# Filter by FFT and gated feed-forward on one core: the taps of the convolution converted earlier from a buffer of their own, batch 0's last transform stage three iterations sooner

## The chip, the cores and the metric

The kernel runs on one core of a Trainium2 chip. The core has TensorE (PE in the profile, its weight loads PEld), VectorE (DVE), ScalarE (ACT), GpSimd (POOL) and SyncE (SP, which here only issues DMAs); ACT issues some DMAs as well. The metric is the device time of one execution in microseconds (us), lower is better. Before the change it was 1565.62 us, the median of three runs (1565.36 to 1567.5).

## The reference

All data are float32. A batch of 8 sequences of 3136 positions with 256 channels is filtered in the frequency domain, and the result goes through a feed-forward layer whose hidden values are gated by a sigmoid of their own convolution over three positions.

```python
batch, seq, dim, d_ff, kernel = 8, 3136, 256, 1024, 3
X = np.fft.rfft(x, axis=1)
y = np.fft.irfft(X * (filt_r + 1j * filt_i)[None], n=seq, axis=1)

h = np.maximum(y @ w_in, 0.0)
hp = zero-padded h, one position on each side
conv_out = sum(conv_w[k][None, None, :] * hp[:, k:k + seq, :] for k in range(3))
gate = 1.0 / (1.0 + np.exp(-conv_out))
out = (h * gate) @ w_out
```

`w_in`, `conv_w` and `w_out` arrive as float64 and are turned into float32 on the core; `w_in` and `w_out` are then split in a high and a low part.

## The kernel before

The transform of length 3136 = 112 x 28 is done as matrix products. There are two stretches of work.

**The forward stretch** is one loop over `i` (`for i in range(NI)`) with a software pipeline. A batch is cut into 14 pieces p, so there are 112 pieces; call the piece number k (0 to 111). In iteration `i` each engine gets, in this order of the code:

- `filt` of k = i - 17: three products on DVE (L354, L355, L356) and a sum on POOL (L358) that makes the tile z;
- `third` of k = i - 19: PE, z times the table `i1_sb` (L365);
- `first` of k = i - 1: PE, the input piece x times `s1_sb` (L319), for i up to 112;
- `second` of k = i - 16: PE (L342; for the last piece of a batch L345);
- `turn` of k = i - 15: four transposes on PE (L330);
- ACT then copies the PSUM results out: `store` of the third stage (L309, followed by the DMA L311 that ACT issues, which writes it to DRAM), `keep` of the first (L323), `turned_rows` (L335);
- one step of the conversion of the convolution's taps (`csteps`, i = 26 to 33) or of the weights (`wsteps`, from i = 35 on, eight blocks of ten steps). A step is one DVE operation of `to_f32` (L160 to L172), the POOL sum at its end (L174), or the split (ACT L146, POOL L152).

From iteration `done` = 116 on, batch 0's **last stage** runs in the same loop: a load of two rows from DRAM (L198), the product with `m2_sb` on PE (L215) one iteration later, and one more iteration later `last_out`: the high part on ACT (L146) and the low part on DVE (L149), written to the tiles y. There are 14 such pieces, so the loop has 133 iterations. `done` also is the iteration where the pools of the input and of the conversion are closed, so the weights have to be finished by then.

**The gated stretch** follows (iteration m). `inner` (six matmuls, L177 to L179) needs all of batch 0's y. Then come `relu` (ACT L458, L460), `conv` (DVE L465, L466), `gate` (ACT L470, DVE L471), `split_g` (ACT L146, POOL L152), and six iterations later `project` (L491 to L493). The last stage of the other seven batches is spread over this stretch. `inner` writes one of four PSUM buffers `ps_h`, which is free again when L471 of its iteration has read it.

The order on PE, ACT, DVE and POOL is the order of the code (`manual_schedule`). SP's queue is in the order that the scheduler gives it. The DMAs of SP and ACT share eight completion semaphores, and an issue waits for the DMA that used its semaphore before.

Input pieces are loaded seven ahead (`XBUFS`). The filter tables and `i1_sb` are loaded piece by piece in iterations 10 to 23 of SP's order (L252 to L256), the taps (L274) in iteration 26, the first two blocks of weights (L269) in iteration 30. The taps' buffer is one of the two `raw` buffers that the blocks of weights use. The loop gives `csteps` eight turns, of which the first three pass without an operation; so five of the eight operations of `to_f32` run on the taps.

## Time and profile before

| | |
|---|---|
| median of three runs | 1565.62 us |
| the profiled execution's own time | 1568.01 us |
| its span, first to last instruction | 1566.2 us |
| PE busy | 1541.9 us (98%) |
| DVE busy | 1288.1 us (82%) |
| ACT busy | 1246.0 us (80%) |
| POOL busy | 704.9 us (45%) |
| mean granted TensorE clock | 0.997 |
| first `inner` of the gated stretch | 377.9 us after the span's start |

A row of a timeline has the start, the duration, engine, line, operation, the tiles (out<-in) and shapes, the count, and in brackets the idle time of the engine just before, with what ended it. A row by windows has for each engine the busy time in that window, then the granted clock (PEclk), the busy share of the DMA engines and what they moved. L12 is line 12 of the kernel.

### The profile page before, as it was taken

Reading aid. Unit: us, or ns where it says so; the run is one execution under the profiler, and the core shown is the slowest. Engines: PE = TensorE matmul, PEld = TensorE weight load, DVE = VectorE, ACT = ScalarE, POOL = GpSimd, SP = SyncE. Lnnn points to the kernel's source line nnn. Section 1 sums busy time; section 2 is a strip of 40 time slices with the busy share of each in tenths; the row PEclk is TensorE's granted clock in tenths of the full one; section 3 lists DMA queues with packets and bytes.
Section 4 is the critical chain, followed back from the end, with each engine's and each line's share of the span. In section 5 each row is a group of like instructions: output and inputs, shape, how many; then the busy total and the mean of one; then the engine's idle time right before and its main releaser. Section 6 shows DMA issues by size and latency. Waiting matters only on the chain.

```text
span 1566.2 us, 27791 instructions
## 1 busy us (share of the span) xinstructions
PE 1541.9 (98%) x10320; PEld 1419.9 (91%) x10320; DVE 1288.1 (82%) x1976; ACT 1246.0 (80%) x2274; POOL 704.9 (45%) x624
## 2 busy tenths in 40 slices
PE   8899999998999999999999999999999999999998
PEld 7677777776999999999999999999999999999998
DVE  3778877888888888888888888888888888888887
ACT  5655555556888888888888888888888888888887
POOL 3345555553444444444444444444444444444444
PEclk9999999999999999999999999999999999999999
DMA  9855555443111011111110111111011110100001
GB/s 233 247 168 167 167 173 168 139 134 106 30 54 48 29 49 48 48 48 45 46 39 22 48 54 48 48 48 48 31 42 48 48 51 28 48 24 24 24 24 48
DMA packets 89062, 115.24 MB, mean 74 GB/s; under 512 B 7400, under 2 KB 60168, under 8 KB 88928
## 3 DMA queue, kind: packets, MB, share of 16 engines
q1 hardware_dynamic: 74592, 87.77, 18.3%
q10 hardware_dynamic: 14336, 25.70, 5.8%
q8 instruction: 82, 1.34, 0.4%
q14 instruction: 52, 0.43, 0.1%
HBM read 62.06 MB, written 51.38 MB: 72 GB/s over the span
## 4 chain that ended last, share of the span: by engine, by line
PE 95%; DMA 2%; DVE 2%; ACT 1%; POOL 0%; issue 0%; SPq 0%; ACTq 0%; POOLq 0%; DVEq 0%
PE ps_h L178 12%; PE ps_h L179 12%; PE ps_h L177 11%; PE po L491 11%; PE po L493 11%; PE po L492 11%; PE ps L365 6%; PE pp L342 6%; PE ps_h L215 6%; PE ps L319 5%; PE ps L330 3%; DMA x<-in_x 1%; DVE y L149 1%; PE ps L215 1%; ACT y L146 1%; PE pp L345 0%
## 5 line engine op out<-in xcount | busy, mean ns | idle before, releaser
L152 POOL TENSOR_TENSOR g<-t,g 128x448 fp32r<-128x448 f32 x448 | 517.8, 1156 | 667.6 <-ACT g L146 264.3
L491 PE MATMUL po<-wo,g 128*128 128x256 f32 x1568 | 441.5, 282 | 0.0
L493 PE MATMUL po<-wo,g 128*128 128x256 f32 x1568 | 433.8, 277 | 0.0
L492 PE MATMUL po<-wo,g 128*128 128x256 f32 x1568 | 433.4, 276 | 0.0
L465 DVE SCALAR_TENSOR_TENSOR t<-ps_h,cw,t 128x448 f32<-128x448 f32 x448 | 305.6, 682 | 83.9 <-ACT t L460 73.2
L178 PE MATMUL ps_h<-y,wi 128*128 128x450 f32 x896 | 330.4, 369 | 4.5 <-DVE y L149 4.5
L177 PE MATMUL ps_h<-y,wi 128*128 128x450 f32 x896 | 328.6, 367 | 3.7 <-ACT y L146 2.0
L179 PE MATMUL ps_h<-y,wi 128*128 128x450 f32 x896 | 328.8, 367 | 0.0
L466 DVE SCALAR_TENSOR_TENSOR t<-ps_h,cw,t 128x448 f32<-128x448 f32 x448 | 306.5, 684 | 16.0
L460 ACT ACTIVATE t<-ps_h,cw 128x448 f32<-128x448 f32 x448 | 285.2, 637 | 43.2 <-ACT ps_h L458 2.6
L491 PEld LDWEIGHTS po<-wo,g 128*128 128x128 f32 x1568 | 294.8, 188 | 7.0
L492 PEld LDWEIGHTS po<-wo,g 128*128 128x128 f32 x1568 | 294.3, 188 | 5.7
L493 PEld LDWEIGHTS po<-wo,g 128*128 128x128 f32 x1568 | 294.5, 188 | 0.0
L458 ACT ACTIVATE ps_h<-ps_h 128x450 f32<-128x450 f32 x448 | 251.8, 562 | 31.5 <-PE ps_h L179 26.7
L471 DVE TENSOR_TENSOR t<-ps_h,t 128x448 f32<-128x448 f32 x448 | 275.3, 615 | 0.1
L470 ACT ACTIVATE t<-t 128x448 f32<-128x448 f32 x448 | 255.0, 569 | 12.1 <-DVE t L466 10.9
L146 ACT ACTIVATE g<-t 128x448 fp32r<-128x448 f32 x448 | 254.5, 568 | 0.2 <-DVE t L471 0.2
L358 POOL TENSOR_TENSOR z<-u,v 120x512 f32<-120x512 f32 x112 | 157.8, 1409 | 187.2 <-DVE v L356 165.0
L179 PEld LDWEIGHTS ps_h<-y,wi 128*128 128x128 f32 x896 | 168.3, 188 | 13.9
L177 PEld LDWEIGHTS ps_h<-y,wi 128*128 128x128 f32 x896 | 170.1, 190 | 12.0 <-ACT y L146 3.0
L178 PEld LDWEIGHTS ps_h<-y,wi 128*128 128x128 f32 x896 | 168.3, 188 | 13.6 <-DVE y L149 6.8
L149 DVE TENSOR_TENSOR y<-ps_h,y 128x448 fp32r<-128x448 f32 x98 | 103.2, 1053 | 75.8 <-ACT y L146 75.8
(53 smaller groups left out, 1658.1 us busy)
## 6 DMA issues: line engine op xcount, KB each, us to landing
x<-in_x SPq DMA_DIRECT2D x112, 224.0 KB, 4.9
b_dram<-sb ACTq DMA_DIRECT2D x112, 224.0 KB, 2.5
br<-b_dram SPq DMA_DIRECT2D x112, 224.0 KB, 2.6
out<-ot SPq DMA_DIRECT2D x27, 896.0 KB, 4.1
raw<-in_w_in SPq DMA_DIRECT2D x8, 256.0 KB, 4.0
raw<-in_w_out SPq DMA_DIRECT2D x8, 256.0 KB
t_sb<-in_fr SPq DMA_DIRECT2D x15, 112.0 KB
t_sb<-in_fi SPq DMA_DIRECT2D x14, 112.0 KB
```

Source lines behind the costliest of these rows:

```text
L146: nc.scalar.activation(dst, src, AF.Copy)
L152: nc.gpsimd.tensor_tensor(out=dst, in0=src, in1=hi.bitcast(F32), op=ALU.subtract)
L177: nc.tensor.matmul(ps, lhsT=wh, rhs=rh, start=start, stop=False, **kw)
L178: nc.tensor.matmul(ps, lhsT=wh, rhs=rl, start=False, stop=False, **kw)
L179: nc.tensor.matmul(ps, lhsT=wl, rhs=rh, start=False, stop=stop, **kw)
L460: nc.scalar.activation(t, h[:, 1:SUB + 1], AF.Copy, scale=cw[:, 1, f:f + 1])
L465: nc.vector.scalar_tensor_tensor(out=t, in0=h[:, 0:SUB], scalar=cw[:, 0, f:f + 1], in1=t, op0=ALU.mult, op1=ALU.add)
L466: nc.vector.scalar_tensor_tensor(out=t, in0=h[:, 2:SUB + 2], scalar=cw[:, 2, f:f + 1], in1=t, op0=ALU.mult, op1=ALU.add)
L471: nc.vector.tensor_mul(t, h[:, 1:SUB + 1], t)
L491: nc.tensor.matmul(o, lhsT=gh[:, sl], rhs=wo[0][:, f], start=first, stop=False, skip_group_check=True)
L492: nc.tensor.matmul(o, lhsT=gh[:, sl], rhs=wo[1][:, f], start=False, stop=False, skip_group_check=True)
L493: nc.tensor.matmul(o, lhsT=gl[:, sl], rhs=wo[0][:, f], start=False, stop=last, skip_group_check=True)
```

## The change

- The taps get a buffer of their own (`rawc`); their load moves from iteration 26 to iteration 8 of SP's order, and their conversion from iterations 26 to 33 to 14 to 21. All eight operations of `to_f32` now run on them.
- The blocks of weights 0 and 1 are loaded in iterations 25 and 27 instead of 30, and their conversion starts at i = 30 instead of 35.
- `done` goes from 116 to 113: batch 0's last stage starts three iterations sooner, and the loop has 130 iterations. The third stage of the last piece (k = 111) no longer fits in it. It is put into the gated stretch behind `inner` of m = 1, with PSUM from `ps_h`; its z, its two table slices (`i1_end`, one more DMA) and its output buffer are kept in a small pool `rest`.
- The tiles `a` go from three buffers to two and `sb` from four to three.

```diff
+    END = NP * B - 1
+    rest = ctx.enter_context(tc.tile_pool(name="rest", bufs=1))
+    i1_end = rest.tile([120, 2, 112], F32, name="i1_end")
+    z_end = rest.tile([120, 2, D], F32, name="z_end")
+    sb_end = rest.tile([112, 2, D], F32, name="sb_end")
+
+    def store(b, p, ps, st):
+        nc.scalar.activation(st, ps, AF.Copy)
+        v = b_dram[b].rearrange("n (r g) d -> (n r) g d", g=G)
+        nc.scalar.dma_start(out=v[:, 2 * p:2 * p + 2], in_=st)
+
+    def third(ps, tables, z):
+        for j in range(2):
+            nc.tensor.matmul(ps[:, j], lhsT=tables[:, j], rhs=z[:, j], start=True, stop=True)
...
         def convert_conv():
             n = 3 * NF
-            raw = cv.tile([128, 2, 512], I32, name="raw")
-            nc.sync.dma_start(out=raw[:, 0, 0:2 * n], in_=conv_w)
-            for _ in range(3):
-                yield
             em = cv.tile([128, 2, 512], I32, name="em", bufs=1)
-            yield from to_f32(cw.rearrange("p k f -> p (k f)"), raw[:, 0, 0:2 * n], em[:, 0, 0:n], em[:, 1, 0:n])
+            yield from to_f32(cw.rearrange("p k f -> p (k f)"), raws.pop("cw"), em[:, 0, 0:n], em[:, 1, 0:n])
...
-            r = fp.tile([112, 2, D], F32, name="a", bufs=3)
+            r = fp.tile([112, 2, D], F32, name="a", bufs=2)
...
-            z = fp.tile([120, 2, D], F32, name="z", bufs=3)
+            z = z_end if (b, p) == at(END) else fp.tile([120, 2, D], F32, name="z", bufs=3)
...
-        done = NP * B + 4
+        done = NP * B + 1
...
                 if i == 8:
                     nc.sync.dma_start(out=eye_sb, in_=eye)
                     nc.sync.dma_start(out=s2_sb, in_=s2[:, 0:120])
+                    raws["cw"] = cv.tile([128, 6 * NF], I32, name="rawc", bufs=1)
+                    nc.sync.dma_start(out=raws["cw"], in_=conv_w)
...
+                if i == 24:
+                    nc.sync.dma_start(out=i1_end, in_=i1[:, G - 2:G])
...
-                    store(*at(m - 4), pt)
+                    store(*at(m - 4), pt, fp.tile([112, 2, D], F32, name="sb", bufs=3))
...
-                if 26 <= i < 34:
+                if 14 <= i < 22:
                     next(csteps, None)
-                if i == 30:
-                    load_weights(0)
-                    load_weights(1)
-                if i >= 35:
+                if i in (25, 27):
+                    load_weights((i - 25) // 2)
+                if i >= 30:
                     next(wsteps, None)
...
+            if m == 1:
+                pt = ps_h.tile([128, 512], F32, name="ps_h")[0:112].rearrange("p (n d) -> p n d", n=2)
+                third(pt, i1_end, z_end)
             if a := at(m - PLAG):
                 project(*a)
...
+            if m == 1:
+                store(B - 1, NP - 1, pt, sb_end)
```

What the change does to the order on three queues is shown below; the line numbers of the changed kernel differ (L160 to L174 are the same in both; L354 to L356 became L359 to L361, L304 became L315, L269 became L285, L365 became L238).

DVE at iterations 29 to 31, before. The three rows of a `filt` are followed by one row of a conversion; `em<-raw 128x24` is the taps.

```order
L354 TENSOR_TENSOR u<-pp,t_sb 120x512
L355 TENSOR_TENSOR v_98<-pp,t_sb 56x512
L356 TENSOR_TENSOR v_98<-pp,t_sb 56x512
L160 TENSOR_SCALAR em<-raw 128x24
L354 TENSOR_TENSOR u<-pp,t_sb 120x512
L355 TENSOR_TENSOR v_99<-pp,t_sb 56x512
L356 TENSOR_TENSOR v_99<-pp,t_sb 56x512
L162 TENSOR_SCALAR em<-raw 128x24
```

And now; `em<-raw 128x512` is block 0 of the weights.

```order
L359 TENSOR_TENSOR u<-pp,t_sb 120x512
L360 TENSOR_TENSOR v_104<-pp,t_sb 56x512
L361 TENSOR_TENSOR v_104<-pp,t_sb 56x512
L359 TENSOR_TENSOR u<-pp,t_sb 120x512
L360 TENSOR_TENSOR v_105<-pp,t_sb 56x512
L361 TENSOR_TENSOR v_105<-pp,t_sb 56x512
L160 TENSOR_SCALAR em<-raw 128x512
L359 TENSOR_TENSOR u<-pp,t_sb 120x512
L360 TENSOR_TENSOR v_104<-pp,t_sb 56x512
```

The first operation on the taps stood between `filt` of piece 12 and of piece 13. It is gone from there, and the first operation on the weights now stands between `filt` of piece 13 and of piece 14.

SP's queue at the end of the filter tables' loads, before:

```order
L256 DMA i_sb<-in_i 120x224
L304 DMA x<-in_x 112x512 x3
L274 DMA raw<-in_conv_w 128x48
L304 DMA x<-in_x 112x512 x4
L269 DMA raw<-in_w_in 128x512
L269 DMA raw<-in_w_out 128x512
```

And now:

```order
L272 DMA i_sb<-in_i 120x224
L315 DMA x<-in_x 112x512
L410 DMA i_end<-in_i 120x224
L315 DMA x<-in_x 112x512
L285 DMA raw<-in_w_in 128x512
L285 DMA raw<-in_w_out 128x512
L315 DMA x<-in_x 112x512 x2
L285 DMA raw<-in_w_in 128x512
```

Block 0 of the weights stands behind two input pieces where it stood behind seven, and the taps' load, which stood behind three, is no longer there.

PE at the border of the two stretches, before (`y` and `wi` are the operands of `inner`):

```order
L345 MATMUL pp<-a,s2s_sb 120x256
L215 MATMUL ps<-m_sb,br 128x112 x4
L365 MATMUL ps<-z,i_sb 112x256 x2
L215 MATMUL ps<-m_sb,br 128x112 x4
L365 MATMUL ps<-z,i_sb 112x256 x2
L215 MATMUL ps<-m_sb,br 128x112 x4
L365 MATMUL ps<-z,i_sb 112x256 x2
L215 MATMUL ps<-m_sb,br 128x112 x4
L177 MATMUL ps_h<-y_3398,wi_72 128x450
```

And now (the row with `x4` is the third stage of pieces 109 and 110; between it and the last row shown stand the twelve matmuls of `inner` of m = 0 and 1, of which three are shown):

```order
L350 MATMUL pp<-a,s2s_sb 120x256
L215 MATMUL ps<-m_sb,br 128x112 x4
L238 MATMUL ps<-z,i_sb 112x256 x4
L177 MATMUL ps_h<-y_3345,wi_72 128x450
...
L178 MATMUL ps_h<-y_3346,wi_72 128x450
L179 MATMUL ps_h<-y_3345,wi_73 128x450
L238 MATMUL ps_h<-z_end,i_end 112x256 x2
```

Three products of the last stage no longer stand behind the last `second`, and the last third stage stands behind the second `inner`. On ACT its copy and the issue of its store stand between the `relu` of m = 0 and that of m = 1.

## The prediction

> **What bounds the kernel now.** I read the page first, then the granted clock by windows, then PE's timeline at the two places where it idles, and last the engines that PE waits for there.

> ```profile
> span 1566.2 us, 27791 instructions
> ...
> PE 1541.9 (98%) x10320; PEld 1419.9 (91%) x10320; DVE 1288.1 (82%) x1976; ACT 1246.0 (80%) x2274; POOL 704.9 (45%) x624
> ...
> PE 95%; DMA 2%; DVE 2%; ACT 1%; POOL 0%; issue 0%; SPq 0%; ACTq 0%; POOLq 0%; DVEq 0%
> ```

> PE is busy 98% of the span and is 95% of the chain. The change takes no matmul away, so all it can win is PE's idle time, 1566.2 - 1541.9 = 24.3 us, and matmuls that run at half clock. Half clock shows in two places (columns: window; length and PE busy; PEld, DVE, ACT, POOL; PEclk, DMA share, GB/s):

> ```profile
> 70.00:72.60 2.60, 2.41 (x14) 1.75 (x14) 0.89 (x3) 0.65 (x2) 0.00 (x0) 1.00 1.03 327
> 72.60:75.50 2.90, 0.03 (x2) 0.03 (x1) 2.77 (x5) 0.60 (x1) 1.26 (x1) 0.89 0.96 333
> 75.50:82.00 6.50, 6.50 (x20) 4.86 (x21) 4.21 (x9) 1.33 (x3) 2.53 (x2) 0.53 0.51 155
> ...
> 376.00:379.00 3.00, 0.54 (x2) 0.26 (x2) 1.85 (x2) 1.79 (x2) 0.00 (x0) 0.94 0.53 156
> 379.00:382.00 3.00, 3.00 (x8) 2.70 (x9) 0.00 (x0) 0.76 (x2) 0.00 (x0) 0.50 0.01 3
> ```

> Both follow a stretch in which PE hardly ran. The first, in PE's timeline:

> ```profile
> 70.19 1.12 PE L319 MATMUL ps<-s_sb,x 112*128 112x112 f32 x8 [0.71 <-DMA x<-in_x]
> ...
> 72.01 0.60 PE L330 MATMUL ps<-eye_sb,turn 128*112 128x128 f32 x4
> 75.48 2.05 PE L365 MATMUL ps<-z,i_sb 120*112 120x256 f32 x4 [2.87 <-POOL z L358]
> ...
> 81.57 1.08 PE L365 MATMUL ps<-z,i_sb 120*112 120x256 f32 x4
> ```

> An undisturbed iteration takes 3.05 us, from one L319 of the chain to the next:

> ```profile
> 85.70 0.88 PE ps L319 x8
> ...
> 88.75 0.88 PE ps L319 x8
> ```

> DVE's timeline tells why z is late there:

> ```profile
> 65.64 0.69 DVE L356 TENSOR_TENSOR v<-pp,t_sb 56x512 f32<-56x512 f32 x1
> 71.65 0.18 DVE L160 TENSOR_SCALAR em<-raw 128x24 int32<-128x24 int32 x1 [5.32 <-DMA raw<-in_conv_w]
> 71.86 0.69 DVE L354 TENSOR_TENSOR u<-pp,t_sb 120x512 f32<-120x512 f32 x1
> ...
> 89.72 0.43 DVE L160 TENSOR_SCALAR em<-raw 128x512 int32<-128x512 int32 x1
> ```

> DVE stood 5.32 us before the first operation on the taps, and the products of piece 13 were queued behind it. The second place is the border between the stretches, where PE waits for z, then for y's high part from ACT, then for its low part from DVE:

> ```profile
> 370.82 1.12 PE L365 MATMUL ps<-z,i_sb 120*112 120x256 f32 x4 [1.07 <-POOL z L358]
> ...
> 373.88 1.12 PE L365 MATMUL ps<-z,i_sb 120*112 120x256 f32 x4 [1.05 <-POOL z L358]
> ...
> 377.86 0.47 PE L177 MATMUL ps_h<-y,wi 128*128 128x450 f32 x1 [1.98 <-ACT y L146]
> 378.93 0.74 PE L178 MATMUL ps_h<-y,wi 128*128 128x450 f32 x1 [0.61 <-DVE y L149]
> ...
> 386.11 0.47 PE L177 MATMUL ps_h<-y,wi 128*128 128x450 f32 x1 [0.81 <-DVE t L471]
> ```

> **The taps and the weights (term A).** Without the wait, L365 would have followed the transposes. Four of them take 0.44 us of PE (0.60 with their drain), so at 72.45; it came at 75.48, 3.03 us late. From there to the next L365 at 81.57 are 6.09 us instead of 3.05, because of the half clock: another 3.04. What the place costs now is 6.07 us.

> The taps no longer hold DVE there. But one iteration later the first operation on the weights stands in front of piece 14's products, and it needs both halves of block 0. When do these land? SP's queue before:

> ```profile
> 65.82 1.27 SPq L304 DMA_DIRECT2D x<-in_x  x3
> 67.51 0.35 SPq L274 DMA_DIRECT2D raw<-in_conv_w  x1
> ```

> and the sizes, in KB per DMA:

> ```profile
> x<-in_x SPq DMA_DIRECT2D x45, 224.0 KB, 4.9
> ...
> i_sb<-in_i SPq DMA_DIRECT2D x14, 105.0 KB, 5.1
> ...
> raw<-in_w_in SPq DMA_DIRECT2D x2, 256.0 KB
> ...
> raw<-in_conv_w SPq DMA_DIRECT2D x1, 24.0 KB
> ```

> The input piece issued at 65.82 ended PE's wait at 70.19, so the queue is some 4.4 us deep. Two more pieces and the taps (472 KB, 483 thousand bytes) came until 71.65: 1.46 us, which is 331 GB/s and agrees with the 327 of the window. In the change, behind that same piece stand the extra table slice, one piece and both halves of block 0 (w_out is as large as w_in): 105 + 224 + 512 = 841 KB, 2.6 us at 327 GB/s, so 72.8. A store of 224 KB that ACT issues in this time costs 0.7 more if it is served ahead, so 73.5 at the latest. I take the middle, 73.1. Then come 0.45 for the operation on 512 columns (0.43 and a gap), and from the first product to L365 what it took before, 75.48 - 71.86 = 3.62: z of piece 14 is there at 77.2. PE would want it one iteration after 72.45, at 75.5. The wait does not go, it **moves by one iteration and shrinks** from 3.0 to 1.7 us (1.4 to 2.1).

> Does the clock fall again? A 2.87 us gap lost it; the gaps of 1.07 and 1.05, with 2 us of matmuls between, did not. 1.7 lies between, nearer to those that kept it; I take no loss, and 3.0 us for the range.

> [...]

> Moving the taps' load to iteration 8 adds 24 KB to a queue that PE waits on at that time (0.1 us), or one issue (0.35 by its row), and three small operations of 0.2 us in front of the first z tiles. A later wait for x absorbs part of it. I take 0.3 lost, with 0 and 0.6 as bounds. The blocks of weights fall in iterations in which DVE has room: 3 x 0.72 + 0.69 = 2.85 of 3.05 us. **A = 6.07 - 1.7 - 0.3 = 4.1 us.** With two buffers for `a` and three for `sb` I see no new wait: an `a` is read by `second` one iteration before ACT writes that buffer again, and a store has three iterations, 9 us, for landings of at most 4.1:

> ```profile
> DMA to landing us min/median/max: 2.2/2.5/4.1
> ```

> **The border (term B).** PE's iterations without and with the last stage:

> ```profile
> 327.96 1.03 PE L365 MATMUL ps<-z,i_sb 120*112 120x256 f32 x4
> ...
> 330.20 1.03 PE L365 MATMUL ps<-z,i_sb 120*112 120x256 f32 x4
> ...
> 334.69 1.03 PE L365 MATMUL ps<-z,i_sb 120*112 120x256 f32 x4
> ...
> 337.82 1.03 PE L365 MATMUL ps<-z,i_sb 120*112 120x256 f32 x4
> ```

> and DVE's low parts, the first, the one of iteration 128, and the last two:

> ```profile
> 341.70 1.01 DVE L149 TENSOR_TENSOR y<-ps,y 128x448 fp32r<-128x448 f32 x1 [2.80 <-ACT y L146]
> ...
> 372.40 0.98 DVE L149 TENSOR_TENSOR y<-ps,y 128x448 fp32r<-128x448 f32 x1
> ...
> 377.03 1.85 DVE L149 TENSOR_TENSOR y<-ps,y 128x448 fp32r<-128x448 f32 x2 [2.06 <-ACT y L146]
> ```

> From the first low part on, DVE is the engine that sets the pace: (372.40 - 341.70) / 10 = 3.07 us an iteration, 0.02 more than PE. Before, iteration 117 is the first with L215 (334.69 to 337.82, 3.13 us, against 2.24 without), and the first low part starts 3.88 us after the L365 of iteration 118. In the change that is iteration 114, whose L365 stands at 327.96: the next L365 at 331.09, the first low part at 334.97, and the fourteenth, 13 x 3.07 us later, at 374.9. It ends at 375.9, against 377.03 + 1.85 = 378.88 before. `inner` can go on 3.0 us sooner.

> What it costs stands behind `inner` of m = 1. PE does the last third stage there (0.87 us, only moved). ACT's copy waits for it, and with the issue of its store holds ACT as the same pair does now:

> ```profile
> 375.03 0.60 ACT L309 ACTIVATE sb<-ps 112x512 f32<-112x512 f32 x1 [1.08 <-PE ps L365]
> ...
> 376.01 1.79 ACT L146 ACTIVATE y<-ps 128x448 fp32r<-128x448 f32 x2 [0.39 <-ACT sb L309]
> ```

> That is 376.01 - 375.03 = 0.98. The `relu` of m = 1 is queued behind it and starts 0.87 + 0.98 = 1.8 us later; so does the L471 behind it, and `inner` of m = 4, which waited for it at 386.11, waits again. **B = 3.0 - 1.8 = 1.2 us**, if the clock falls as it did. PE still idles there: piece 110's z now comes behind two more low parts, some 2.0 us after PE has done piece 109, and the low part keeps PE 1.4 us more, with 1.2 us of matmuls between. That is much like the 1.98 and 0.61 that lost the clock, so I let it fall. If it stays up, the fill of the gated stretch is some 1.4 us shorter: from 379 to 382 eight matmuls ran in 3.00 us, which at full clock take 8 x 0.205 = 1.6.

> **The sum.** A + B = 4.1 + 1.2 = 5.3 us; the profiled execution took 1568.01 us (span 1566.2 and 1.8 around it), so 1562.7 for such a one. It lies 2.4 above the median of the timed runs. The timed runs differ by 2.1 us among themselves, about the price of one stretch at half clock (3.0 and 1.4), so some of what I remove may be missing from the median one; I take 0.5 us off the gain for that: 1565.62 - 4.8 = **1560.8 us**.

> **Rivals.**
> 1. The moved wait loses the clock as well. For it: the windows show only that 1.07 keeps and 2.87 loses. Then A is 4.1 - 3.0 = 1.1, the sum 2.3, the time 1563.3: within what can be told from no change.
> 2. The moved wait does not come, because block 0 lands by 71.5 (two issues later than the taps did, so against it: the queue's 4.4 us), or the clock holds at the border. The first gives 1.7 more, the second 1.4, both together 5.3 + 3.1 = 8.4, so 1559 to 1557.2.
> 3. Slower: DVE stays blocked by the weights much longer than I reckon. 1 MB of weights now goes out while the input is still being caught up; if the second block and the stores are served ahead of w_out, z of piece 14 comes late by as much. The loss starts where the new wait exceeds 6.07 - 0.3 + 1.2 = 7.0 us with its clock, so from a landing of 73.1 + (7.0 - 3.0 - 1.7) = 75.4 on. With 512 KB more and two stores (960 KB, 3.0 us) plus a landing that is 1.5 us slower it is 77.6 us: 2.2 us slower than now, 1567.8; beyond that it is seen as slower. Against it: the queue is served in order in the rows above.
> 4. The border gives nothing. The change says that batch 0's last stage ends sooner, but the two waits there, 2.0 and 1.4 us, may cost the half clock twice instead of once: B = 1.2 - 1.4 = -0.2, the sum 3.9, the time 1562.2. For it: 3.4 us of idle time in some 4.6. Against it: before, 4.7 us of idle time in some 9 cost it once.

> **Chances.** Forecast 0.47, rival 1 0.24, rival 2 0.18, rival 4 0.06, rival 3 0.05. The range from rival 2's far end to past rival 1 is 1557.3 to 1564.2; it leaves out rival 3 and little of the rest. A measurement of this kernel tells about 0.2%, 3.1 us, from no change. Faster by more: most of the forecast (0.43), rival 2 (0.18), a part of rivals 4 (0.04) and 1 (0.05), so 0.70; within: 0.26; slower: 0.04, nearly all of rival 3.

> **What would show it.** Right: DVE idles some 4 to 5 us before L160 of a 128x512 tile, <-DMA raw, one iteration later than now; PE's L238 idles 1 to 2 us <-POOL z there with PEclk 1.00 behind it; the last L149 ends some 3 us earlier against the third stages around it; `relu` of m = 1 stands behind the copy of `sb_end`. Wrong: no idle before that L160; PEclk 0.5 after it; or new waits for x or `sb` between 15 and 85 us.

## The result: 22.6 us slower, and where the time went

| | before | changed |
|---|---|---|
| median of the timed runs, us | 1566.21 | 1588.81 |
| all timed runs, us | 1565.36 to 1567.5 | 1585.14 to 1589.78 |
| ratio, 95% interval | | 1.0139 (1.0121 to 1.0157) |
| span of the profiled execution, us | 1566.2 | 1588.0 |

The forecast was 1560.8 us, 4.8 faster. Of the timed runs of the experiments below one, of e13, took 1915.41 us at a mean granted clock of 0.753; its ratio leaves it out. The page of the changed kernel:

```profile
span 1588.0 us, 27800 instructions
...
PE 1564.0 (98%) x10320; PEld 1441.0 (91%) x10320; DVE 1292.1 (81%) x1978; ACT 1246.8 (79%) x2274; POOL 704.6 (44%) x625
```

Against the page before, PE's busy time has grown by 1564.0 - 1541.9 = 22.1 us, with the same 10320 matmuls. Its idle time is what it was: 1588.0 - 1564.0 = 24.0, before 24.3. So no wait explains the loss. From the first `inner` of m = 10 to the end of the span it is 1165.5 us before and 1186.0 changed, so 20.5 of the 21.8 us lie behind that point and 1.25 ahead of it. The matmuls themselves take longer, and the groups by line show which ones. Those of `project`, before:

```profile
L491 PE MATMUL po<-wo,g 128*128 128x256 f32 x1568 | 441.5, 282 | 0.0
L493 PE MATMUL po<-wo,g 128*128 128x256 f32 x1568 | 433.8, 277 | 0.0
L492 PE MATMUL po<-wo,g 128*128 128x256 f32 x1568 | 433.4, 276 | 0.0
```

and changed:

```profile
L497 PE MATMUL po<-wo,g 128*128 128x256 f32 x1568 | 447.3, 285 | 0.0
L498 PE MATMUL po<-wo,g 128*128 128x256 f32 x1568 | 439.2, 280 | 0.0
L499 PE MATMUL po<-wo,g 128*128 128x256 f32 x1568 | 438.4, 280 | 0.0
```

These durations overlap: a matmul is shown for some 280 ns, and the next one starts long before that. The pace is read from one start to the next. In PE's timeline, the first and the last of one run of twelve before:

```profile
434.62 0.28 PE L491 MATMUL po<-wo,g 128*128 128x256 f32 x1
...
435.87 0.28 PE L493 MATMUL po<-wo,g 128*128 128x256 f32 x1
```

and of one changed:

```profile
431.51 0.28 PE L497 MATMUL po<-wo,g 128*128 128x256 f32 x1
...
432.81 0.28 PE L499 MATMUL po<-wo,g 128*128 128x256 f32 x1
```

Eleven steps take 1.25 us before and 1.30 changed. Over all runs of nine or twelve in the trace the step is 113.5 ns before and 117.9 ns changed (here and below: the mean start-to-start time of a run without its first two steps, then the mean over the runs; the medians over the runs are 113.3 and 117.9). From the fourth step on 445 of the 448 runs have the short step before, and all 448 the long one in the change, at a granted clock of 1.00. There are 3 x 1568 = 4704 such matmuls: 4704 x 4.4 ns = 20.7 us. Summed from start to start from m = 10 on, PE needs 17.8 us more within the runs of `project`, 1.4 from their last matmul to the next `inner`, and 1.1 at `inner`, whose step went from 204.7 to 205.0 ns: 20.3 us.

The change touches neither `project` nor its operands. But its new pool of `i1_end`, `z_end` and `sb_end` takes 896 + 2048 + 2048 = 4992 bytes of every SBUF partition for the whole program, and what is allocated behind it stands 4992 bytes further on. `g` moves from byte 91872 to 96864 of the partition, `t`, `ot` and the odd batches' `y` by as much; the weights `wi` and `wo`, allocated ahead of it, and the even batches' `y`, on the other side, stay. 4992 is 9 x 512 + 384, so `g` went from 224 to 96 modulo 512.

The forward stretch and the border did not bring what was forecast either. At the weights, PE's timeline of the changed kernel:

```profile
75.92 0.60 PE L335 MATMUL ps<-eye_sb,turn 128*112 128x128 f32 x4
79.52 2.05 PE L238 MATMUL ps<-z,i_sb 120*112 120x256 f32 x4 [3.00 <-POOL z L363]
...
85.61 1.14 PE L238 MATMUL ps<-z,i_sb 120*112 120x256 f32 x4
```

and DVE's:

```profile
70.68 0.69 DVE L361 TENSOR_TENSOR v<-pp,t_sb 56x512 f32<-56x512 f32 x1
75.29 0.43 DVE L160 TENSOR_SCALAR em<-raw 128x512 int32<-128x512 int32 x1 [3.92 <-DMA raw<-in_w_out]
```

DVE stood 3.92 us ahead of its first weights, PE 3.00 for the `z` behind them, and the next L238 comes 85.61 - 79.52 = 6.09 us later instead of 3.05: half clock, as before. At the border, PE (the row with `z_end` is the last third stage; the last row is `inner` of m = 4):

```profile
374.44 1.12 PE L238 MATMUL ps<-z,i_sb 120*112 120x256 f32 x4 [1.96 <-POOL z L363]
...
377.03 0.74 PE L178 MATMUL ps_h<-y,wi 128*128 128x450 f32 x1 [1.27 <-DVE y L149]
...
381.32 1.75 PE L238 MATMUL ps_h<-z_end,i_end 120*112 120x256 f32 x4
...
387.32 0.47 PE L177 MATMUL ps_h<-y,wi 128*128 128x450 f32 x1 [1.79 <-DVE t L477]
```

and ACT:

```profile
383.12 0.60 ACT L232 ACTIVATE sb_end<-ps_h 112x512 f32<-112x512 f32 x1 [2.61 <-PE ps_h L238]
...
384.10 0.53 ACT L464 ACTIVATE ps_h<-ps_h 128x450 f32<-128x450 f32 x1 [0.39 <-ACT sb_end L232]
```

The low part that `inner` waits for came at 377.03, before at 378.93: 1.90 us sooner, though the forward stretch was 1.05 us later by then (third stage of iteration 113 at 326.76, before 325.71). With that taken out it is 2.95. Yet `inner` of m = 4 starts at 387.32, before at 386.11. The clock fell at both places (columns as in the prediction; the first row is the window ahead of the fall at the weights, the others belong to the border):

```profile
75.60:79.01 3.41, 0.92 (x6) 0.47 (x4) 3.25 (x6) 0.89 (x2) 0.96 (x1) 1.00 0.92 326
...
372.55:375.97 3.42, 1.33 (x5) 0.81 (x5) 3.33 (x5) 1.93 (x3) 1.28 (x1) 1.00 0.44 133
375.97:379.38 3.41, 2.35 (x6) 2.14 (x7) 0.98 (x1) 0.29 (x2) 1.27 (x1) 0.50 0.22 67
379.38:382.80 3.42, 3.42 (x11) 2.78 (x10) 1.37 (x2) 1.10 (x2) 0.00 (x0) 0.50 0.00 0
```

These stretches are cut where the clock changes; at both places it stayed at half for 6.83 us. Before, it did so for 6.83 us at the weights and for 3.413 at the border, and it fell at 74.84 and at 378.63 us of the span, 89.0 times 3.413 us apart. From the first fall on, each stretch between two changes is a whole number of 3.413 us: 2, 87, 1 and 347 of them before (the last 1184.43 us, so 3.4133 each), 2, 85, 2 and 353 changed. So in these profiles the clock changed on a fixed grid of windows, and what a wait cost depended on how the grid fell on it: the border's waits of 1.98 and 0.61 us lost the clock before, and the same two kept it in e10's profile below.

So there are three questions: whether the addresses make `project` slower, and through what; what each part of the change is worth without that; and whether the wait at the weights is what the early start loses.

### The profile page after: what moved, and what is told of

It reads as the page before. It is cut to its first block, busy times and chain, and to the rows that moved or that the text cites. A ratio compares the mean times of both kernels' runs of the same rounds, so it can differ in the third digit from the quotient of the medians.

```text
span 1588.0 us, 27800 instructions
## 1 busy us (share of the span) xinstructions
PE 1564.0 (98%) x10320; PEld 1441.0 (91%) x10320; DVE 1292.1 (81%) x1978; ACT 1246.8 (79%) x2274; POOL 704.6 (44%) x625
## 4 chain that ended last, share of the span: by engine, by line
PE 94%; DMA 2%; DVE 2%; ACT 1%; issue 0%; POOL 0%; SPq 0%; ACTq 0%; POOLq 0%; DVEq 0%
PE ps_h L178 12%; PE ps_h L179 12%; PE po L497 12%; PE po L498 12%; PE ps_h L177 11%; PE po L499 11%; PE ps_h L215 5%; PE ps L238 5%; PE pp L347 5%; PE ps L324 5%; PE ps L335 3%; PE ps L215 1%; DVE y L149 1%; DMA x<-in_x 1%; DMA b_dram<-sb 0%; ACT y L146 0%
## 5 line engine op out<-in xcount | busy, mean ns | idle before, releaser
L497 PE MATMUL po<-wo,g 128*128 128x256 f32 x1568 | 447.3, 285 | 0.0
L498 PE MATMUL po<-wo,g 128*128 128x256 f32 x1568 | 439.2, 280 | 0.0
L499 PE MATMUL po<-wo,g 128*128 128x256 f32 x1568 | 438.4, 280 | 0.0
L471 DVE SCALAR_TENSOR_TENSOR t<-ps_h,cw,t 128x448 f32<-128x448 f32 x448 | 305.7, 682 | 95.4 <-ACT t L466 85.3
L178 PE MATMUL ps_h<-y,wi 128*128 128x450 f32 x896 | 329.5, 368 | 5.2 <-DVE y L149 5.2
L177 PE MATMUL ps_h<-y,wi 128*128 128x450 f32 x896 | 331.2, 370 | 2.7 <-DVE t L477 2.5
L146 ACT ACTIVATE g<-t 128x448 fp32r<-128x448 f32 x448 | 254.5, 568 | 0.2 <-DVE t L477 0.2
L178 PEld LDWEIGHTS ps_h<-y,wi 128*128 128x128 f32 x896 | 169.8, 189 | 15.7 <-DVE y L149 7.6
L177 PEld LDWEIGHTS ps_h<-y,wi 128*128 128x128 f32 x896 | 169.0, 189 | 10.9 <-DVE t L477 3.6
L149 DVE TENSOR_TENSOR y<-ps_h,y 128x448 fp32r<-128x448 f32 x98 | 103.5, 1056 | 87.0 <-ACT y L146 87.0
## 6 DMA issues: line engine op xcount, KB each, us to landing
x<-in_x SPq DMA_DIRECT2D x112, 224.0 KB, 5.2
br<-b_dram SPq DMA_DIRECT2D x112, 224.0 KB, 2.6
b_dram<-sb ACTq DMA_DIRECT2D x111, 224.0 KB, 2.5
raw<-in_w_in SPq DMA_DIRECT2D x8, 256.0 KB, 3.9
raw<-in_w_out SPq DMA_DIRECT2D x8, 256.0 KB, 5.0
```

Source lines behind the costliest of these rows:

```text
L177: nc.tensor.matmul(ps, lhsT=wh, rhs=rh, start=start, stop=False, **kw)
L178: nc.tensor.matmul(ps, lhsT=wh, rhs=rl, start=False, stop=False, **kw)
L471: nc.vector.scalar_tensor_tensor(out=t, in0=h[:, 0:SUB], scalar=cw[:, 0, f:f + 1], in1=t, op0=ALU.mult, op1=ALU.add)
L497: nc.tensor.matmul(o, lhsT=gh[:, sl], rhs=wo[0][:, f], start=first, stop=False, skip_group_check=True)
L498: nc.tensor.matmul(o, lhsT=gh[:, sl], rhs=wo[1][:, f], start=False, stop=False, skip_group_check=True)
L499: nc.tensor.matmul(o, lhsT=gl[:, sl], rhs=wo[0][:, f], start=False, stop=last, skip_group_check=True)
```

## Experiments on the addresses

### Moving nothing but addresses

Three kernels are the kernel before with an empty buffer put in; one is the changed kernel with 128 bytes more in its new pool.

```diff
 # e1: before, at the place of the change's new pool
+    gap = ctx.enter_context(tc.tile_pool(name="gap", bufs=1))
+    gap.tile([128, 224], F32, name="gap")        # 896 bytes
 # e2: changed
     sb_end = rest.tile([112, 2, D], F32, name="sb_end")
+    rest.tile([128, 32], F32, name="gap")        # 128 bytes
 # e3, e4: before, between y_odd and wp (the pool of t, g and ot)
+    gap = ctx.enter_context(tc.tile_pool(name="gap", bufs=1, reuse_waits="tile"))
+    gap.tile([128, 224], F32, name="gap")        # e4: 96, so 384 bytes
     wp = ctx.enter_context(tc.tile_pool(name="wp", bufs=2, reuse_waits="tile"))
```

> The kernel before with 896 bytes per partition left empty where the change puts its three end buffers (4992 bytes); 4992 - 4096 = 896, so every buffer behind it (y_odd, t, g, ot) has the same address modulo 4096 as in the changed kernel, and no instruction differs. Theory H1 (the pace of the project matmuls hangs on the place of their operands in SBUF): 117.9 ns from matmul to matmul instead of 113.5, page row of the first project line about 447 us in place of 441.5, and 1586 +- 2 us. Rival H2 (PSUM slots, since the changed kernel's last third stage takes a slot of ps_h) and rival H3 (the instruction stream): 113.5 ns and 1566 +- 1 us.

> The changed kernel with 128 bytes per partition left empty behind its three end buffers: buffers behind them stand 5120 = 10 x 512 bytes after their place before. H1, if the place counts modulo 512: 113.5 ns from one project matmul to the next and 1567 +- 1.5 us (the 20 us of the slower project gone, the 1 us lost in the forward stretch and at the border kept). H1, if it counts modulo more than 512: between 113.5 and 117.9 ns. H2 and H3: 117.9 ns and 1588 us.

> The kernel before with 896 bytes left empty between y_odd and the buffers t, g and ot: only these three move, by the same 896 bytes modulo 4096 as in the changed kernel. H1 through g, t or ot: 117.9 ns and 1587 +- 2 us. H1 through y_odd (which only inner reads) or H2, H3: 113.5 ns and 1566 +- 1 us.

> As the run before, with 384 bytes in place of 896: the same place of g modulo 512 (96 bytes), another modulo 1024. H1 modulo 512 or less: 117.9 ns, 1587 +- 2 us, as with 896. H1 modulo 1024 or more: another pace than with 896. H2, H3: 113.5 ns and 1566 +- 1 us.

| | step in `project`, ns | time, us | before beside it, us |
|---|---|---|---|
| e1, before + 896 bytes | 117.9 | 1590.4 | 1566.44 |
| e2, changed + 128 bytes | 113.4 | 1568.74 | 1566.44 |
| e3, before, `t`, `g`, `ot` + 896 | 117.8 | 1591.9 | 1566.44 |
| e4, before, `t`, `g`, `ot` + 384 | 117.8 | 1593.1 | 1566.44 |

The groups by line of e1, which has the instructions of the kernel before:

```profile
L493 PE MATMUL po<-wo,g 128*128 128x256 f32 x1568 | 447.3, 285 | 0.0
L494 PE MATMUL po<-wo,g 128*128 128x256 f32 x1568 | 439.1, 280 | 0.0
```

and of e2, which has those of the change:

```profile
L498 PE MATMUL po<-wo,g 128*128 128x256 f32 x1568 | 441.5, 282 | 0.0
L500 PE MATMUL po<-wo,g 128*128 128x256 f32 x1568 | 433.8, 277 | 0.0
```

An empty buffer gives the unchanged kernel the whole loss (24.0 us in a single run), and 128 bytes take it from the changed one: ratio 1.0016 (1.0006 to 1.0026), so 2.3 us slower than before in place of 22.6. The difference of 20.3 us agrees with the sum above. From m = 10 to the end e1's trace takes 1186.1 us and e2's 1165.4: the two kernels have changed places. It is neither the PSUM slots nor the instructions; `t`, `g` and `ot` suffice, and 384 does what 896 does. What is left of the change is 2.3 us slower, not 4.8 faster.

### Which buffer, and against what

Each of the four buffers of `g` gets its own place, so that one run shows four of them: hidden group f uses buffer f mod 4.

```diff
-            gs[j, f] = [wp.tile([128, 2 * SUB], F32R, name=f"g{h}", bufs=4) for h in range(2)]
+            gs[j, f] = [gp[2 * (f % 4) + h].tile([128, 2 * SUB], F32R, name=f"g{h}") for h in range(2)]
 # gp: a pool for each, with gaps between. Places of g0 and g1 modulo 512:
 # e5: (352, 352) (480, 480) (0, 0) (160, 160)
 # e6: (224, 96) (96, 224) (224, 352) (352, 224)
```

> The kernel before with its four buffers of g (the pair g0, g1 of hidden group f lies in buffer f mod 4) laid out one by one, so that in one run the project matmuls of f = 0, 1, 2, 3 (and 4 to 7 again) read g at 352, 480, 0 and 160 bytes modulo 512 (before: 224; changed: 96). Nothing else that project reads moves. Theory G (g alone, through its place modulo 256): f = 1 at 113.3 ns as 224, f = 0 at 117.9 as 96, and 0 and 160 new. Theory G512 (modulo 512): the four differ without that pair rule. Rival T (the place of t or ot, which moved with g in the runs so far): 113.3 ns for all four.

> As the run before, with g0 and g1 apart: (224, 96), (96, 224), (224, 352), (352, 224) bytes modulo 512 for f mod 4 = 0 to 3. Of three project matmuls two load g0 as weights and one g1. If each weight load pays for its own place: with g0 at 96 two of three steps long (about 116.4 ns mean), with g1 at 96 one of three (about 114.8). If it is the distance of g0 and g1 from one another: f = 0 and 1 alike. Rival T: 113.3 ns for all four.

Median over the runs of the mean step in ns, for f = 0 to 7, worked out from the starts in the trace:

```
e5  117.9  113.6  117.8  119.0  117.9  113.3  119.0  119.2
e6  113.3  114.7  113.3  116.9  113.3  119.2  113.3  114.2
```

In e5 (1583.5 us) only the second buffer, at 480, is fast; 480 and 224, the place before, are alike modulo 256. `t` has not moved there, and `ot` has its place modulo 512 as before, so it is `g`. In e6 (1576.2 us) it is less plain. Where `g0`, the weights of two matmuls in three, is at 224 (f = 0, 2, 4, 6), 56, 38, 42 and 47 of the 56 runs are fast from their fourth step on, though `g1` is not at its old place. Where `g0` is at 96 or 352 (f = 1, 3, 5, 7), 33, 28, 20 and 56 are, and single runs are of one of two kinds. These are the steps in ns of four runs of f = 1:

```
119 118 121 113 113 114 113 113 114 113 113
119 118 120 114 113 113 114 113 113 114 113
201 114 120 117 124 119 117 118 118 117 125
202 114 119 118 124 118 118 118 118 117 124
```

Which kind a run is shows in its first steps. None went over from the short steps to the long ones there. Of the 128 of e6 with long steps from the fourth to the sixth, 27 went over to the short ones, as in this one of f = 2: 201 120 118 117 119 121 116 114 114 113 113. None of the expectations describes this, the mean of long and short steps by weight least of all: `project` has two paces, and a run falls into one of them near its start.

Then the weights were moved instead, with `g` at 224 throughout.

```diff
-    wo = [wc.tile([128, NF, D], F32R, name=f"wo{h}") for h in range(2)]
+    for f, place in enumerate([416, 448, 480, 0, 32, 64, 96, 128]):   # modulo 512
+        gap(place)
+        for h in range(2):
+            wo[h, f] = wc.tile([128, D], F32R, name=f"wo{h}_{f}")
 # and wi in the same way, by pairs of hidden groups, at 160, 224, 288, 352
```

> The kernel before with g0 and g1 all at 224 bytes modulo 512 as before, but the projection's weights wo cut into one piece for each hidden group f, at 160, 192, 224, 0, 32, 64, 96, 128 bytes modulo 256 for f = 0 to 7 (before: 160 for all); nothing else of the computation changes. Theory R (the distance of g from wo modulo 256 counts, g being loaded while wo streams): f = 0 (distance 64) at 113.3 ns, f = 4 (distance 192, that of the changed kernel) and f = 2 (0) and f = 7 (96, as 0 and 352 in the run with four places of g: 96, 192) at 117.9 to 119. Rival A (the place of g by itself): 113.3 ns for all f. [...]

Mean step in ns while the even batches' `y` is read (e9 took 1588.3 us), for f = 0 to 7, with the place of `wo` and the distance from it to `g`, modulo 256:

```
wo        160    192    224      0     32     64     96    128
distance   64     32      0    224    192    160    128     96
step    114.4  117.9  119.4  116.8  117.8  119.9  118.9  117.6
```

`g` stands still, and the pace changes with `wo`: its place alone isn't what counts. Of the eight distances at steps of 32 bytes only 64 is fast, which is that of the kernel before. The distance from `wo` to `y` changes here too. The odd batches, whose `y` was at 192 in this run, help to tell the two apart: f = 1, whose `wo` has the place of `y` as in the kernel before, is slow (118.2 ns), and f = 0, where only the distance from `wo` to `g` is the old one, is fast (114.2). The `wi` read ahead of them differed as well. `inner` went between 203.8 and 206.8 ns with its own distances.

Last, the operands were moved together.

```diff
 # e12: before, ahead of wi, so that wi, wo, y_odd, t, g and ot move by 128 bytes
+    wc.tile([128, 32], F32, name="gap")
 # e14: before, ahead of the even batches' y, which alone moves by 128 bytes
+    ctx.enter_context(tc.tile_pool(name="gapr", bufs=1, side="right", reuse_waits="tile")).tile([128, 32], F32, name="gap")
 # e15: both
```

> The kernel before with 128 bytes left empty ahead of the weights: wi, wo and all that lies behind them moves, so that wo lies at 32 and g at 96 bytes modulo 256 (before 160 and 224; the changed kernel 160 and 96). The distance from wo to g is 64 as before. Theory R (only the distance counts): 113.3 ns and 1566 +- 2 us. Rival A2 (each place counts by itself: g at 96 was slow wherever it stood so far, wo at 32 too): 117.9 ns and 1587 us.

> The kernel before with 128 bytes left empty ahead of the y of the even batches, which alone moves (from 160 to 32 bytes modulo 256; y of the odd batches, wi and wo stay at 160, g at 224). In the run with wo, wi, g and the odd y moved together, project took 113.4 ns in odd batches and 117.1 in even ones, whose y had stayed. Theory RY (the distance of y from the weights counts too, since inner's last matmuls run into project's first): project 117 ns in even batches, 113.4 in odd ones, about 1576 us. Rival (it was the place of wo or g after all): 113.4 ns in all batches, 1566 +- 2 us.

> The run with wo, wi, g and the odd y moved by 128 bytes, and y of the even batches moved by 128 too: all distances modulo 256 are those of the kernel before, all places other. Theory R with RY (distances alone count): 113.4 ns in all batches, 1566 +- 2 us. Rival A2 (places count by themselves): 117 ns in even batches as without it, 1578 us.

| | step, even batches, ns | step, odd batches, ns | time, us |
|---|---|---|---|
| e12, all but the even `y` moved | 117.2 | 113.4 | 1578.9 |
| e14, the even `y` moved alone | 117.2 | 113.4 | 1576.7 |
| e15, all moved | 113.8 | 113.7 | 1568.8 |

The kernel before took 1566.83 us beside e12 and 1568.98 beside e14 and e15.

e12 answered neither of its two theories: odd batches kept the fast pace and even ones lost it. That led to e14 and e15. The groups by line of e14 between 400 and 500 us, which lies in an even batch:

```profile
L493 PE MATMUL po<-wo,g 128*128 128x256 f32 x126 | 35.3, 280 | 0.0
L494 PE MATMUL po<-wo,g 128*128 128x256 f32 x126 | 35.3, 280 | 0.0
```

and between 540 and 660 us, in an odd one:

```profile
L494 PE MATMUL po<-wo,g 128*128 128x256 f32 x158 | 43.7, 277 | 0.0
L493 PE MATMUL po<-wo,g 128*128 128x256 f32 x158 | 43.7, 276 | 0.0
```

280 and 276 ns are the two paces, in one run, by the place of a buffer that `project` doesn't read. `y` is what `inner` streams, and `inner` runs into `project`: in the changed kernel's PE timeline one last matmul of `inner` starts at 505.36 and is shown for 0.37 us, and the first of `project` starts at 505.56. With every distance kept and every place moved (e15), the pace is back to within 0.3 ns, and the time to that of before. So what decided here is distances between the operands of neighbouring matmuls, modulo 256 bytes: from `wo` to `g` (e9: 114.4 ns at 64 bytes, 116.8 to 119.9 at the seven others), and from `y` to one or more of the others (e14: 117.2 ns where `y` alone had moved, 113.4 where it had not); `y` was not tried against each of them, and not every move of it mattered (f = 0 of e9 above). Why the distances count, no run shows.

## Experiments on the parts of the change

### Each part alone, with the addresses kept

e7 has the taps' buffer and the early start of taps and weights, and nothing of the border. e8 has the border's part with the 128 bytes of padding, and the taps as before; its weights must start two iterations sooner to end in time.

```diff
 # e7: before, with the change's hunks for raws["cw"], the taps at 14 <= i < 22,
 #     load_weights at i in (25, 27) and the weights' steps from i >= 30
 # e8: changed + 128 bytes, with these four hunks taken back, but
-                if i >= 30:
+                if i >= 33:
```

> The kernel before with the taps' own buffer and the earlier start of taps and weights alone; border and all addresses as before. By the trace of the changed kernel, where the forward stretch ended 1.05 us later: +1.0, 1567.2 us, and 113.3 ns in project. By the prediction's term A: -4.1, 1562.1 us. Theory P (the half-clock windows stand on a grid that runs free of the program, so what a wait costs differs from run to run): mean granted clock spread over 0.995 to 1.000 within the runs, and the times in step with it, 1.1 us for each 3.41 us window.

> The kernel before with the border's part of the change alone (last stage three iterations sooner, last third stage in the gated part), with 128 bytes of padding that keep g's place modulo 512, taps as before, weights converted from iteration 33 on (they must end before the earlier border). By the trace of the changed kernel: -0.2 saved, 1566.4 us. By the prediction's term B: -1.2, 1565.0 us. Theory P adds: a second half-clock window in more of the runs than before, about +1.1 us for each.

e7: 1566.0 us against 1566.83, ratio 0.9995 (0.9986 to 1.0005). e8: 1568.24, ratio 1.0009 (0.9999 to 1.0018). So the taps and weights gave 0.8 us and the border took 1.4, both within what can be told from nothing; neither gave what was forecast (4.1 and 1.2).

The expectation on the windows came true. In the 59 timed runs of the kernel before that stand beside e1 to e13 the mean granted clock lies between 0.995 and 1.000, and the time goes with it: the four at 1.000 have a median of 1563.9 us, the four at 0.995 one of 1569.0. A window of 3.413 us at half clock takes 3.413 x 0.5 / 1567 = 0.0011 off the mean clock, so about one us goes with each. The mean clock over the runs was 0.9975 for the kernel before, 0.9978 for e7 and 0.9954 for e8 (0.9957 for e2, the whole change): about two lowered windows more with the border's part.

### The weights' first step later, and the last third stage later

e10 is e7 with the weights' conversion from iteration 33 in place of 30; e13 is the whole change with padding and the same edit; e11 is e13 with the last third stage, its copy and its store at m = 12.

```diff
 # e10, e11, e13
-                if i >= 30:
+                if i >= 33:
                     next(wsteps, None)
 # e11, both places
-            if m == 1:
+            if m == 12:
```

> Taps and weights as changed, border as before, but the weights' conversion from iteration 33 in place of 30, so that VectorE meets its first weights when they have landed (in the changed kernel it waited 3.92 us for them and PE 3.00 for z). Theory W (that wait, and the half-clock window which it brings, is all that the early start loses): about 3.0 us for the wait and up to 3.4 for two windows of the changed kernel's profile gone, 1562 +- 1.5 us. Rival (the early z waits of 0.2 to 0.4 us and the windows elsewhere eat it): 1565 to 1566 us, as with iteration 30 (1566.0).

> The changed kernel with 128 bytes of padding, weights' conversion from iteration 33, and the last third stage with its copy and store at m = 12 of the gated part in place of m = 1. Theory F (at the border ACT's copy ahead of relu of m = 1 keeps PE short of work while its pipeline fills, and brings a second half-clock window): against the run with only the weights moved 1.2 to 3.0 us faster, so about 1560 us. Rival (the border's windows come from its waits for z and y whatever stands behind them): 1.4 us slower than that run, as the border alone was against before, 1563.5 us.

> The changed kernel with 128 bytes of padding and the weights' conversion from iteration 33; the last third stage stays at m = 1. Theory F (the copy ahead of relu of m = 1 is what the border loses): 1.2 to 3 us slower than with the last third stage at m = 12 (1562.6), so 1564 to 1565.5 us. Rival (the place of the last third stage makes no difference): 1562.6 +- 1 us.

| | time, us | ratio to before, 95% interval | mean clock of the runs |
|---|---|---|---|
| e10, taps and weights, from 33 | 1562.35 | 0.9971 (0.9961 to 0.9981) | 0.9993 |
| e11, whole change, from 33, third stage at m = 12 | 1562.62 | 0.9972 (0.9962 to 0.9981) | 0.9978 |
| e13, whole change, from 33, padded | 1562.47 | 0.9971 (0.9959 to 0.9983) | 0.9965 |

e10's DVE at the place where it stood 3.92 us:

```profile
78.63 0.69 DVE L352 TENSOR_TENSOR v<-pp,t_sb 56x512 f32<-56x512 f32 x1
79.35 0.43 DVE L160 TENSOR_SCALAR em<-raw 128x512 int32<-128x512 int32 x1
```

and its PE:

```profile
77.36 1.03 PE L361 MATMUL ps<-z,i_sb 120*112 120x256 f32 x4
...
80.41 1.03 PE L361 MATMUL ps<-z,i_sb 120*112 120x256 f32 x4
```

The wait is gone, and the iterations take their 3.05 us. That is worth 1566.0 - 1562.35 = 3.7 us against e7 (each beside its own runs of before), and all three kernels beat the one before, by 4.5 us by their ratios. Theory W holds in its time, not in its "all": the waits for `z` at the taps (0.28, 0.36 and 0.37 us in e10's profile) are still there.

Theory F falls: the last third stage at m = 1 or at m = 12 makes no difference. What the border does shows against e10, which has the border of before. PE in e10 (the last row is `inner` of m = 4):

```profile
369.56 1.12 PE L361 MATMUL ps<-z,i_sb 120*112 120x256 f32 x4 [1.05 <-POOL z L354]
373.54 0.47 PE L177 MATMUL ps_h<-y,wi 128*128 128x450 f32 x1 [1.98 <-ACT y L146]
374.61 0.47 PE L178 MATMUL ps_h<-y,wi 128*128 128x450 f32 x1 [0.61 <-DVE y L149]
...
380.48 0.47 PE L177 MATMUL ps_h<-y,wi 128*128 128x450 f32 x1 [0.89 <-DVE t L468]
```

and in e13:

```profile
368.01 1.12 PE L239 MATMUL ps<-z,i_sb 120*112 120x256 f32 x4 [1.95 <-POOL z L364]
...
370.61 0.74 PE L178 MATMUL ps_h<-y,wi 128*128 128x450 f32 x1 [1.28 <-DVE y L149]
...
381.06 0.47 PE L177 MATMUL ps_h<-y,wi 128*128 128x450 f32 x1 [1.75 <-DVE t L478]
```

The low part comes 4.0 us sooner in e13, 1.0 of which the forward stretch had brought in that execution. From there to m = 4 are 10.45 us instead of 5.87: two windows at half clock from 369.94 on, and the third stage with its copy. In e10's profile the clock never fell between 11.4 us and the end of the span. What the earlier end saves, the clock and the fill take back: 1562.47 and 1562.35. The runs' mean clock says the same, 0.9965 and 0.9993, about two and a half windows.

## Why the prediction was wrong

**The step that failed is its first.** "The change takes no matmul away, so all it can win is PE's idle time ... and matmuls that run at half clock" takes a matmul's duration as given by its shape. The new pool's size was never set against the addresses behind it; only new waits were looked for in the buffers. `project` slowed from 113.5 to 117.9 ns, 20.3 us by the sum of the steps and as much by the run with the padding. None of the rivals has this mechanism, and the range ended 24.6 us below the result.

**Term A, forecast 4.1, in the profile of the change about -1.0, alone 0.8 (-0.8 to 2.2).** The wait moved by one iteration, as forecast, to DVE's first operation on the weights. It was mis-sized, 3.00 us in place of 1.7, because the second half of block 0 was there at 75.29 and not at 73.1. SP issued that half only at 70.15, after some 0.6 us of waiting for a store to land:

```profile
68.68 0.32 SPq L315 DMA_DIRECT2D x<-in_x  x1
69.04 0.43 SPq L285 DMA_DIRECT2D raw<-in_w_in  x1
70.15 0.35 SPq L285 DMA_DIRECT2D raw<-in_w_out  x1
```

and the queues did not reach the 327 GB/s reckoned with (last column of the windows):

```profile
69.00:72.00 3.00, 3.00 (x19) 2.13 (x17) 2.07 (x3) 2.38 (x5) 0.91 (x2) 1.00 0.90 267
72.00:75.30 3.30, 3.30 (x21) 2.60 (x20) 0.01 (x1) 1.74 (x3) 0.81 (x1) 1.00 0.86 291
```

The clock fell as well (rival 1), another 3.04. That depends on the execution: in the profiles of e2 and e7, which have the same early start, PE waited 2.45 and 2.04 us there and the clock stayed up. The wait lay across two windows, busy for 79% and 50% in e2 and for 62% and 78% in e7. And the early loss was 1.1, not 0.3: three small operations on the taps took 1.14 us each instead of 0.18, each ending with a `z` of POOL that had started before it, and PE waited for three tiles of `z` there, 0.37, 0.36 and 0.37 us. One of the three, on DVE:

```profile
32.41 1.14 DVE L168 SCALAR_TENSOR_TENSOR cw<-em 128x24 f32<-128x24 int32 x1
```

and the `z` beside it, on POOL, until 33.51:

```profile
32.12 1.39 POOL L363 TENSOR_TENSOR z<-u,v 120x512 f32<-120x512 f32 x1 [2.73 <-DVE v L361]
```

6.07 - 3.00 - 3.04 - 1.1 = -1.07, which is the 1.05 us by which the forward stretch was later. That the place was worth 6.07 us was right: without the wait (e10, as rival 2 has it) the forecast's terms give 6.07 - 0.3 = 5.8, or 5.0 with the early loss as measured, and 4.5 (3.0 to 6.1) was found.

**Term B, forecast 1.2, alone -1.4 (-2.8 to 0.2), on top of e10 0.** "`inner` can go on 3.0 us sooner" was right, 2.95. Not right was that the clock falls once, as before. It fell for two windows in the profile of the change, which is rival 4 with its -0.2; that rival had 0.06. Over all profiles the old border (twelve kernels) lowered none to two windows, the new one (five) two or three; that it fell for a single window in the profile of before was the luck of that execution. The prediction looked at single gaps (1.07 keeps, 2.87 loses); in the profiles the fall went with the busy share of a whole window on the grid. The window before the fall was busy for 1.33 of 3.42 us (39%), the one at the weights for 0.92 of 3.41 (27%). In the 17 profiles together 28 windows at full clock were followed by half clock; PE was busy for 47% or less of each. No busier window lowered it; the least busy of those, in e2, was busy for 1.69 of 3.41 us.

**The signs to look for** were partly right: DVE idle before L160 of 128x512, 3.92 us for "4 to 5"; the last low part three us earlier; `relu` of m = 1 behind the copy of `sb_end`. L238 idled 3.00 us for "1 to 2", and PEclk was 0.50 behind it, which was named as a sign of being wrong. None of them looks at the matmuls of `project`, which hold nearly all of the change in time. One slip of the sums changes nothing: rivals 1 and 2 leave out the 0.5 us that the forecast and rival 4 take off the gain.

## What to carry to other kernels

The new pool, which lives through the whole program, moved all that is allocated behind it by 4992 bytes, and `project`, which keeps TensorE busy, went from 113.5 to 117.9 ns a matmul, 3.9% more; in e1 an empty buffer of 896 bytes did the same alone. After a change to buffers, compare the mean duration of the same matmul in both profiles first, and hold addresses fixed (here 128 bytes of padding) before judging what the change was meant to do. A wait ahead of TensorE cost more than its length where the clock fell behind it: at the weights of the changed kernel 3.00 us of waiting left a window busy for 0.92 of 3.41 us, and the half clock took another 3.04. That wait went when VectorE's first operation on the data was put later (the start at iteration 33), and not when they were only loaded sooner.
